# Routing of the first mixture of experts: one plan of seven digits for all experts, and counting in pairs of token columns

## The chip, the cores and the metric

The kernel runs on one core of one Trainium2 chip. The metric is the time of one execution on the device, in microseconds (us).

## The reference

The program is a chain of three parts: attention in chunks, a mixture of experts with balanced routing, and a second mixture with the two best experts per token. The change is in the routing of the first mixture, on 3072 tokens and 8 experts that take 384 tokens each:

```python
logits = x @ w_gate                       # 3072 x 8
order = np.argsort(-logits.flatten())
for idx in order:                         # best pairs of token and expert first
    tok, e = idx // E, idx % E
    if assigned[tok] >= 0 or counts[e] >= cap:   # cap = 384
        continue
    assigned[tok] = e
    counts[e] += 1
for e in range(E):
    mask = assigned == e
    out[mask] = np.maximum(x[mask] @ w1[e], 0.0) @ w2[e]
```

## The kernel before

**Stages.** Attention runs from 0 to some 112 us and leaves the logits `L` in SBUF: token n lies in partition n % 128 and column n // 128, so a tile has `G` = 24 columns of 128 tokens, for each of `E` = 8 experts. Then the first mixture runs expert by expert (`moe1`): `mm1` multiplies the expert's 384 gathered tokens by `w1` in three half-precision passes (products `m<-xT,w_...`), and for the first five experts `mm2_f32` multiplies by `w2` in single precision (products `m2f<-st,hT`). The second mixture (`moe2`) follows.

**Order of the work.** The order is written out when the kernel is built. `Pipe` keeps a modelled time for each engine; the main products call `tick()` between them, and generators (routing, lists, gathers, weight splits) that have come due by the modelled time issue their instructions there. `pipe.due` tells the splits of weights on VectorE when the routing wants VectorE next. Each engine then takes its instructions in that order, and waits in it. If a thing that the main products need isn't ready by the model, spare products `m<-ones` are put in.

**Routing.** `route` (a generator) finds, expert by expert, which expert fills up next, and at which logit. The logit is found digit by digit, as a number in bits. A round for digit s: VectorE compares the best logit `V` of each token with the candidates of the digit (`GE`, a 0/1 table of 24 columns by `nj` candidates); TensorE multiplies `GE` with the one-hot table `OH` of the tokens' best experts and so counts, for each candidate and expert, the tokens above (`cross`); VectorE compares the counts with the places left (`capB`, the flag `fl`); TensorE sums the flags over the candidates and spreads the sum to all partitions (`dg`); VectorE takes the largest (`d`) and makes the next candidates `ci`.

There are two plans. `FAST` has seven digits of 4, 3, 5, 5, 5, 5 and 5 bits and one token column per product: 24 products with 8 moving columns each. Expert 0 (which has its first two digits from a histogram made during attention, so five rounds are left) and expert 1 (seven rounds) use it. `THRIFTY` has eight digits of 4 bits and eight token columns per product: 3 products with 120 stationary and 64 moving columns, of which only the diagonal blocks are wanted. ScalarE evicts the result to `blk`, and eight products with slices of the identity add the blocks up. Experts 2 to 6 use it. Expert 7 needs no rounds. In the trace all PSUM tiles of the routing are called `rps`, and the flags `flf` (FAST) and `flt` (THRIFTY).

When an expert's threshold is known, `lists1` writes its list of tokens (`l1pos`, `slps`, `idx`), `gather1` fetches the rows by an indirect DMA on GpSimd's queue, and they are transposed, for experts 0 and 1 by TensorE (`tps`). Weights of expert k are fetched once its number is known (`est`), and split into two halves by ScalarE and VectorE. Nearly all instructions show line 68, the helper that records them, so they are told apart by their tiles.

Of the kernel before, what the change touches and what calls it, by code (L numbers as in the profile page):

```python
# [8 lines left out]
F32 = mybir.dt.float32  # L9
# [17 lines left out]
G = NTOK // 128  # L27
# [28 lines left out]
class Eng:  # L56


    def __init__(self, eng, pipe, name):
        self._a = (eng, pipe, name)  # L60
# [543 lines left out]
class Plan:  # L604


    def __init__(self, name, bits, cols):
        self.name, self.cols = name, cols
        self.shifts = [sum(bits[i + 1 :]) for i in range(len(bits))]
        self.nj = [(1 << b) - 1 for b in bits]  # L610
        self.off = [sum(self.nj[1:i]) for i in range(1, len(bits) + 1)]
# [4 lines left out]
FAST = Plan("f", (4, 3, 5, 5, 5, 5, 5), 1)  # L616
THRIFTY = Plan("t", (4,) * 8, 8)
NJ, NT, NH = 31, 15, 127


def route_setup(ctx, pool):
# [13 lines left out]
    for plan in (FAST, THRIFTY):  # L635
        fl = pool.tile([max(plan.nj), len(plan.nj), E], BF16, name="fl" + plan.name)
        memset(fl, 0.0)
        setattr(ctx, "fl" + plan.name, fl)
    return [
        lambda: memset(ctx.capB, float(CAP)),  # L640
# [123 lines left out]
def route(ctx):  # L764
# [36 lines left out]
    for k in range(E):  # L801
        def tl(shape, dt, n, **kw):
            return pool.tile(shape, dt, tag="rt" + n, name=f"{n}_{k}", **kw)
# [24 lines left out]
        plan = FAST if k < 2 else THRIFTY  # L828
        jtab = getattr(ctx, "jtab" + plan.name)
        off, NS = plan.off, len(plan.nj)  # L830
        FL = getattr(ctx, "fl" + plan.name)
        score = tl([128, E], F32, "score")
        R = tl([128, FAST.off[-1] + 1], I32, "R")[:, : off[-1] + 1]
# [34 lines left out]
        for s in range(s0, NS):  # L868
            nj, o = plan.nj[s], off[s]
            GE = tl([128, G * NJ], F16, "GE")[:, : G * nj].rearrange("p (c j) -> p c j", j=nj)  # L870
            step = G if k else G // 2
            for c in range(0, G, step):
                bc = [128, step, nj]
                V_.tensor_tensor(
                    GE[:, c : c + step], V[:, c : c + step].unsqueeze(2).to_broadcast(bc),
                    cand[:, :nj].unsqueeze(1).to_broadcast(bc), op=ALU.is_ge,
                )
# [14 lines left out]
            g = plan.cols  # L892
            cross = pst([g * nj, E, g])
            for c in range(0, G, g):
                P_.matmul(
                    cross.rearrange("p e c -> p (e c)"), GE[:, c : c + g].rearrange("p c j -> p (c j)"), OH[:, :, c : c + g],
                    start=(c == 0), stop=(c == G - g),
                )
# [7 lines left out]
            cnt = cross[:, :, 0]  # L906
            if g > 1:
                pipe.due = pipe.rdy("s", cross) + 900
                yield pipe.rdy("s", cross) - 200
                blk = tl([NT * THRIFTY.cols, E, THRIFTY.cols], F16, "blk")  # L910
                pipe.S.activation(blk, cross, AF.Copy)
                pipe.due = pipe.rdy("p", blk) + 450
                yield pipe.rdy("p", blk)
                cnt = pst([nj, E])
                for i in range(g):
                    P_.matmul(
                        cnt, ctx.id16[: g * nj, nj * i : nj * i + nj], blk[:, :, i], start=(i == 0), stop=(i == g - 1)
                    )
            pipe.due = pipe.rdy("v", cnt)
            yield pipe.due - 200  # L920
            fl = FL[:nj, s]
            V_.tensor_tensor(fl, cnt, capB[:nj], op=ALU.is_ge)
# [23 lines left out]
            else:  # L946
# [3 lines left out]
                ci = tl([128, NJ], I32, "ci")  # L950
# [94 lines left out]
def constants():  # L1045
# [10 lines left out]
    for plan in (FAST, THRIFTY):  # L1056
        jtab = [np.arange(1, n + 1) << sh for n, sh in zip(plan.nj[1:], plan.shifts[1:])] + [np.zeros(1)]
        f["jtab" + plan.name] = np.tile(np.concatenate(jtab).astype(np.int32), (128, 1))
# [1043 lines left out]
```

## Time and profile before

| | |
|---|---|
| median of 3 runs | 1035.27 us (1031.76 to 1038.93) |
| the profiled execution | 1030.15 us, span 1028.4 us |
| TensorE products busy | 980.4 us, 95% of the span |
| VectorE busy | 639.3 us, 62% |
| ScalarE busy | 466.5 us, 45% |
| GpSimd busy | 283.9 us, 28% |
| mean granted clock of TensorE | 0.980 |

Busy times of TensorE are those of pipelined products: several are under way at once, so what a group of products costs is read from the starts of its neighbours, not from its own duration. In the rows, PE is TensorE (PEld its weight loads), DVE is VectorE, ACT is ScalarE, POOL is GpSimd. A shape such as `128*31 128x8` is 128 rows by 31 stationary columns, with a result of 8 moving columns per row of the moving side.

### The profile page before, as it was taken

What the parts mean: (1) busy time and instruction counts of PE and PEld (TensorE: products, weight loads), DVE (VectorE), ACT (ScalarE), POOL (GpSimd) and SP (SyncE); (2) the same over time, 40 slices, a digit from 0 to 9 for tenths busy, and PEclk for the clock granted to TensorE, in tenths of its full rate; (3) what the DMA queues carried; (4) which work ended last, traced back from release to release, by engine and by line L of the source; (5) the groups of instructions that cost most, each with busy time, mean ns of one, the idle gap of its engine ahead of it and who ended that gap; (6) DMA issues with size and microseconds to landing.
All of it is one profiled execution on the core that took longest, in us unless ns stands there. A gap on an engine that the chain in (4) does not pass through costs nothing. (4 is left out here: it accounts for less than half of the span.)

```text
span 1028.4 us, 21808 instructions
## 1 busy us (share of the span) xinstructions
PE 980.4 (95%) x8278; PEld 590.8 (57%) x8278; DVE 639.3 (62%) x2095; ACT 466.5 (45%) x799; POOL 283.9 (28%) x468
## 2 busy tenths in 40 slices
PE   7988589899999999999989999999999999999997
PEld 5777467676767675545554454555545555555553
DVE  5998776566665958697756845547355464554221
ACT  5776252643461738888225635044161441523110
POOL 3776042010111304030022333133232432332321
PEclk8999689999999999999999999999999999999999
DMA  8888564466858678778187829458186492654410
GB/s 308 299 276 276 195 221 151 129 190 175 229 181 201 166 211 225 232 228 149 37 257 219 244 72 301 84 155 244 62 250 132 117 290 63 182 116 102 123 62 31
DMA packets 146848, 184.61 MB, mean 180 GB/s; under 512 B 105154, under 2 KB 105666, under 8 KB 145204
## 3 DMA queue, kind: packets, MB, share of 16 engines
q1 hardware_dynamic: 129410, 131.73, 45.4%
q0 software_dynamic: 13872, 45.15, 15.1%
q10 hardware_dynamic: 3458, 6.30, 1.7%
q8 instruction: 66, 1.08, 0.5%
q14 instruction: 42, 0.34, 0.1%
HBM read 127.10 MB, written 32.44 MB: 155 GB/s over the span
## 5 line engine op out<-in xcount | busy, mean ns | idle before, releaser
L68 PEld LDWEIGHTS <-hT 128*128 128x128 f16 (+2 forms) x1800 | 143.2, 99 | 158.2 <-issue 2.8
L68 ACT ACTIVATE hT<-m 128x384 f16<-128x384 f32 (+2 forms) x152 | 75.6, 499 | 275.7 <-PE m L68 274.1
L68 DVE SCALAR_TENSOR_TENSOR hT<-m,hT 128x384 f16<-128x384 f32 (+2 forms) x152 | 86.4, 570 | 97.9 <-ACT hT L68 97.8
L68 ACT ACTIVATE junk<-st 128x1024 f16<-128x1024 f32 x108 | 113.6, 1052 | 56.2 <-DMA st<-w_dram 29.0
L68 PE MATMUL m2f<-st,hT 128*128 128x256 f32 x480 | 127.6, 398 | 0.6 <-ACT hT L68 0.6
L68 POOL DMA_INDIRECT out_dram<-pv,ts x47 | 48.6, 1034 | 250.2 <-DVE pv L68 88.7
L68 DVE SCALAR_TENSOR_TENSOR pv<-m,ys,pv 128x512 f32<-128x512 f32 (+2 forms) x47 | 33.5, 714 | 118.3 <-PE m L68 118.2
L68 PE MATMUL m<-xT,w_0h 128*128 128x384 f16 (+2 forms) x384 | 96.6, 331 | 2.9 <-DMA xT<-xg 2.9
L68 PE MATMUL m<-xT,w_2h 128*128 128x384 f16 (+2 forms) x384 | 97.7, 334 | 1.7 <-DVE hT L68 1.7
L68 PE MATMUL m<-xT,w_3h 128*128 128x384 f16 (+2 forms) x384 | 96.7, 332 | 0.0
L68 PE MATMUL m<-xT,w_1h 128*128 128x384 f16 (+2 forms) x384 | 96.5, 331 | 0.0
L68 PEld LDWEIGHTS m2f<-st,hT 128*128 128x128 f32 x480 | 83.3, 190 | 10.2 <-ACT hT L68 1.0
L68 PE MATMUL m<-w_3h,hT 128*128 128x512 f16 (+2 forms) x300 | 71.6, 345 | 1.4 <-DVE hT L68 1.4
L68 PE MATMUL m<-w_0h,hT 128*128 128x512 f16 (+2 forms) x300 | 72.1, 346 | 0.0
L68 PE MATMUL m<-w_1h,hT 128*128 128x512 f16 (+2 forms) x300 | 71.5, 345 | 0.0
L68 PE MATMUL m<-w_2h,hT 128*128 128x512 f16 (+2 forms) x300 | 71.5, 345 | 0.0
L68 PE MATMUL m<-xT,w_2l 128*128 128x384 f16 (+2 forms) x192 | 64.2, 334 | 0.0
L68 PE MATMUL m<-xT,w_1l 128*128 128x384 f16 (+2 forms) x192 | 63.6, 331 | 0.0
L68 PE MATMUL m<-xT,w_3l 128*128 128x384 f16 (+2 forms) x192 | 63.5, 331 | 0.0
L68 PE MATMUL m<-xT,w_0l 128*128 128x384 f16 (+2 forms) x192 | 63.5, 331 | 0.0
L68 POOL DMA_INDIRECT xg<-x,rows x54 | 54.2, 1004 | 28.1 <-issue 12.7
L68 POOL DMA_INDIRECT pv<-out_dram,tg x47 | 46.5, 990 | 55.1 <-DMA out_dram<-pv,ts 39.0
(350 smaller groups left out, 1829.3 us busy)
## 6 DMA issues: line engine op xcount, KB each, us to landing
st<-w_dram SPq DMA_DIRECT2D x64, 512.0 KB
st<-x_dram SPq DMA_DIRECT2D x64, 512.0 KB
v<-vctx_dram SPq DMA_DIRECT2D x24, 520.0 KB
k<-kT_dram SPq DMA_DIRECT2D x24, 312.0 KB
xr<-rb SPq DMA_DIRECT2D x24, 264.0 KB
x<-rb SPq DMA_DIRECT2D x24, 264.0 KB
q<-qT_dram SPq DMA_DIRECT2D x12, 512.0 KB
out_dram<-zero ACTq DMA_DIRECT2D x24, 256.0 KB
```

Of the source, the lines that this page charges most:

```text
L68: return f(*args, **kw)
```

## The change

The plans become one, the seven digits of `FAST`, for all experts. Token columns are counted in pairs: the candidates of a column lie 32 apart in a constant tile `GE`, so that a pair is a stationary side of 64 columns (31 candidates, one unused, 31 candidates, one unused) and a moving side of 16. Twelve such products add up in one PSUM tile of 64 rows. Rows 0 to 30 at the even columns hold the counts of the even token columns, rows 32 to 62 at the odd ones those of the odd token columns. VectorE adds the two in the test: `need` is the places left less the odd counts, and the flag is whether the even counts reach `need`. ScalarE's eviction `blk` and the eight products that add the blocks go.

```diff
-FAST = Plan("f", (4, 3, 5, 5, 5, 5, 5), 1)
-THRIFTY = Plan("t", (4,) * 8, 8)
-NJ, NT, NH = 31, 15, 127
+PLAN = Plan((4, 3, 5, 5, 5, 5, 5))
+NT, NH, PAIR = 15, 127, 32
...
+    ctx.fl = pool.tile([max(PLAN.nj), len(PLAN.nj), E], BF16, name="fl")
+    memset(ctx.fl, 0.0)
+    ctx.GE = pool.tile([128, G, PAIR], F16, name="GE")
     return [
+        lambda: memset(ctx.GE, 0.0),
...
-        plan = FAST if k < 2 else THRIFTY
-        jtab = getattr(ctx, "jtab" + plan.name)
+        plan, jtab, FL = PLAN, ctx.jtab, ctx.fl
...
-            GE = tl([128, G * NJ], F16, "GE")[:, : G * nj].rearrange("p (c j) -> p c j", j=nj)
+            GE = ctx.GE
             step = G if k else G // 2
             for c in range(0, G, step):
                 bc = [128, step, nj]
                 V_.tensor_tensor(
-                    GE[:, c : c + step], V[:, c : c + step].unsqueeze(2).to_broadcast(bc),
+                    GE[:, c : c + step, :nj], V[:, c : c + step].unsqueeze(2).to_broadcast(bc),
                     cand[:, :nj].unsqueeze(1).to_broadcast(bc), op=ALU.is_ge,
                 )
...
-            g = plan.cols
-            cross = pst([g * nj, E, g])
-            for c in range(0, G, g):
+            cross = pst([2 * PAIR, E, 2])
+            flat = cross.rearrange("p e c -> p (e c)")
+            for c in range(0, G, 2):
                 P_.matmul(
-                    cross.rearrange("p e c -> p (e c)"), GE[:, c : c + g].rearrange("p c j -> p (c j)"), OH[:, :, c : c + g],
-                    start=(c == 0), stop=(c == G - g),
+                    flat, GE[:, c : c + 2].rearrange("p c j -> p (c j)"), OH[:, :, c : c + 2],
+                    start=(c == 0), stop=(c == G - 2),
                 )
...
-            cnt = cross[:, :, 0]
-            if g > 1:
-                pipe.due = pipe.rdy("s", cross) + 900
-                yield pipe.rdy("s", cross) - 200
-                blk = tl([NT * THRIFTY.cols, E, THRIFTY.cols], F16, "blk")
-                pipe.S.activation(blk, cross, AF.Copy)
-                pipe.due = pipe.rdy("p", blk) + 450
-                yield pipe.rdy("p", blk)
-                cnt = pst([nj, E])
-                for i in range(g):
-                    P_.matmul(
-                        cnt, ctx.id16[: g * nj, nj * i : nj * i + nj], blk[:, :, i], start=(i == 0), stop=(i == g - 1)
-                    )
-            pipe.due = pipe.rdy("v", cnt)
+            pipe.due = pipe.rdy("v", cross)
             yield pipe.due - 200
-            fl = FL[:nj, s]
-            V_.tensor_tensor(fl, cnt, capB[:nj], op=ALU.is_ge)
+            fl, need = FL[:nj, s], tl([PAIR, E], F32, "need")[:nj]
+            odd = slice(PAIR, PAIR + nj)
+            V_.scalar_tensor_tensor(need, cross[odd, :, 1], -1.0, capB[odd], op0=ALU.mult, op1=ALU.add)
+            V_.tensor_tensor(fl, cross[:nj, :, 0], need, op=ALU.is_ge)
```

The table of candidates in the constants (`jtab`) is stored once in place of twice.

## Rows read from the trace of the kernel before

**Rows 1.** Busy time by stretch: length, then each engine's busy us, clock, DMA.

```profile
107.00:110.00 3.00, 2.00 (x20) 1.90 (x19) 0.87 (x5) 2.54 (x7) 0.00 (x0) 1.00 1.04 392
111.00:126.00 15.00, 6.42 (x134) 5.04 (x134) 13.29 (x56) 1.95 (x3) 2.08 (x13) 0.50 0.37 139
143.00:383.00 240.00, 236.11 (x1883) 163.70 (x1882) 159.90 (x679) 106.92 (x208) 36.71 (x87) 1.00 0.62 177
```

**Rows 2.** Waits of TensorE after 143 us: us in total, times, longest.

```profile
PE tps L68 <- DMA xg<-xr,idx: 2.6, 1, 2.6
...
PE rps L68 <- ACT blk L68: 0.7, 1, 0.7
```

**Rows 3.** Timeline of TensorE, second half of an expert: start us, us, instructions.

```profile
231.21 1.97 PE L68 MATMUL m2f<-st,hT 128*128 128x256 f32 x8
...
236.41 0.30 PE L68 MATMUL rps<-OH,GE 128*120 128x64 f16 x3
236.55 1.11 PE L68 MATMUL m2f<-st,hT 128*128 128x256 f32 x4
...
239.05 1.56 PE L68 MATMUL m2f<-st,hT 128*128 128x256 f32 x6
240.45 0.30 PE L68 MATMUL rps<-OH,GE 128*120 128x64 f16 x3
```

**Rows 4.** The same timeline in the first half of expert 0, during expert 1's routing.

```profile
148.35 0.33 PE L68 MATMUL m<-xT,w_1l 128*128 128x384 f16 x1
...
148.84 0.33 PE L68 MATMUL m<-xT,w_1l 128*128 128x384 f16 x1
149.10 0.80 PE L68 MATMUL rps<-OH,GE 128*31 128x8 f16 x24
149.83 0.50 PE L68 MATMUL m<-xT,w_1h 128*128 128x384 f16 x2
...
150.74 0.17 PE L68 MATMUL rps<-flf,onesb 31*128 31x8 bf16 x1
150.85 0.34 PE L68 MATMUL m<-xT,w_1l 128*128 128x384 f16 x1
```

**Rows 5.** The same timeline in the first half of expert 1, during expert 2's routing.

```profile
198.65 0.30 PE L68 MATMUL rps<-OH,GE 128*120 128x64 f16 x3
...
202.17 0.30 PE L68 MATMUL rps<-OH,GE 128*120 128x64 f16 x3
```

**Rows 6.** Instructions on the tile blk: count, ns min/median/max, first and last start.

```profile
L68 ACT ACTIVATE blk<-rps x40: 201/223/224, 177.2 to 373.6; 120x64 f16<-120x64 f32 x40
```

**Rows 7.** Timeline of TensorE in the second mixture, first products of 64 columns.

```profile
520.98 0.59 PE L68 MATMUL m<-w_3h,hT 128*128 128x512 f16 x2
521.41 0.38 PE L68 MATMUL m<-w_3l,hT 128*128 128x512 f16 x1
521.72 0.41 PE L68 MATMUL m<-w_0h,hT 128*64 128x256 f16 x4
```

**Rows 8.** Timeline of weight loads, histogram of expert 0, 127 columns.

```profile
108.59 0.32 PEld L507 LDWEIGHTS <-ge 128*127 128x127 f16 x4
110.58 0.18 PEld L507 LDWEIGHTS <-ge 128*127 128x127 f16 x1 [1.68 <-DVE ge L500]
111.32 0.40 PEld L507 LDWEIGHTS <-ge 128*127 128x127 f16 x3 [0.56 <-issue]
```

**Rows 9.** Timeline of all engines in a routing round of expert 0.

```profile
115.53 0.19 DVE L68 SCALAR_TENSOR_TENSOR ci<-d,R 128x31 int32<-128x31 int32 x1
...
115.75 1.00 DVE L68 TENSOR_TENSOR GE<-V,ci 128x372 f16<-128x372 f32 x2
...
116.36 0.95 PE L68 MATMUL rps<-OH,GE 128*31 128x8 f16 x24 [1.06 <-DVE GE L68]
```

**Rows 10.** Timeline of TensorE in the first half of expert 5.

```profile
393.92 0.76 PE L68 MATMUL slps<-slr,sloh 128*32 128x12 f16 x24
...
396.66 0.48 PE L68 MATMUL m<-xT,w_2h 128*128 128x384 f16 x2 [1.72 <-DVE hT L68]
```

More of the change, by code (lines that the diff above doesn't have):

```diff
@@ L604, with __init__ @@
 class Plan:
-    def __init__(self, name, bits, cols):
-        self.name, self.cols = name, cols
+    def __init__(self, bits):
         self.shifts = [sum(bits[i + 1 :]) for i in range(len(bits))]
@@ L634, in route_setup @@
     memset(ctx.left, float(CAP))
[L635 to L638, printed above, removed]
+    ctx.fl = pool.tile([max(PLAN.nj), len(PLAN.nj), E], BF16, name="fl")
+    memset(ctx.fl, 0.0)
+    ctx.GE = pool.tile([128, G, PAIR], F16, name="GE")
     return [
+        lambda: memset(ctx.GE, 0.0),
         lambda: memset(ctx.capB, float(CAP)),
@@ L827, in route @@
             return
-        plan = FAST if k < 2 else THRIFTY
-        jtab = getattr(ctx, "jtab" + plan.name)
+        plan, jtab, FL = PLAN, ctx.jtab, ctx.fl
         off, NS = plan.off, len(plan.nj)
-        FL = getattr(ctx, "fl" + plan.name)
         score = tl([128, E], F32, "score")
-        R = tl([128, FAST.off[-1] + 1], I32, "R")[:, : off[-1] + 1]
+        R = tl([128, off[-1] + 1], I32, "R")
         d = tl([128, 1], I32, "d", bufs=2)
@@ L949, in route @@
                     V_.tensor_reduce(score, dgs.rearrange("p s e -> p e s"), axis=AX.X, op=ALU.add)
-                ci = tl([128, NJ], I32, "ci")
+                ci = tl([128, PAIR], I32, "ci")
                 V_.scalar_tensor_tensor(
@@ L1055, in constants @@
     f["cand0"] = np.tile(np.where(k0 >= 0, k0, k0 ^ 0x7FFFFFFF).astype(np.int32).view(np.float32), (128, 1))
-    for plan in (FAST, THRIFTY):
-        jtab = [np.arange(1, n + 1) << sh for n, sh in zip(plan.nj[1:], plan.shifts[1:])] + [np.zeros(1)]
-        f["jtab" + plan.name] = np.tile(np.concatenate(jtab).astype(np.int32), (128, 1))
+    jtab = [np.arange(1, n + 1) << sh for n, sh in zip(PLAN.nj[1:], PLAN.shifts[1:])] + [np.zeros(1)]
+    f["jtab"] = np.tile(np.concatenate(jtab).astype(np.int32), (128, 1))
     k0 = (np.arange(1, NH + 1, dtype=np.int64) - 64) << 25
```

## The prediction

> **What bounds the kernel now.** I read three views in this order. First the busy time by stretch [rows 1]: from 143 to 383 us, where the first mixture of experts runs beside the routing of experts 1 to 6, TensorE is busy for 236.1 of 240 us at a granted clock of 1.00, VectorE for 159.9 and ScalarE for 106.9. So in that stretch a microsecond of TensorE work is a microsecond of the kernel, and the eviction that the change takes from ScalarE is not what the stretch waits for. From 111 to 126 us the picture is turned round: VectorE is busy for 13.3 of 15 us, TensorE for 6.4 at the lower clock (0.50, 1.2 GHz). That is the routing of expert 0, a chain of short instructions with nothing else to run. Then the waits of TensorE [rows 2]: the routing's own are small, 0.7 us for the eviction `blk`, and 2.6 us for the rows that expert 1's list gathers. Last the order of the instructions on TensorE, to see what one routing round costs the main stream.
>
> **What a round costs TensorE today.** The main products are the yardstick. In the second half of an expert (`m2f`) one takes 0.215 us: eight last 1.97 and four 1.11, so 0.86/4 [rows 3]. From one counting group at 236.41 to the next at 240.45 pass 4.04 us, with 14 `m2f` in them (4, 4 and 6): 4.04 - 14 x 0.215 = 1.03 us are the round's. In the first half (`mm1`) three products start in 0.49 us (148.35 to 148.84), so 0.163 each [rows 4]. From 198.65 to 202.17 there are 17 of them: 3.52 - 2.77 = 0.75 us [rows 5]. The 40 evictions `blk` from 177.2 to 373.6 us [rows 6] mark the rounds of experts 2 to 6 (five of eight); in TensorE's order 23 of them start within `m2f` and 17 within `mm1`: 23.7 + 12.8 = 36.5 us.
>
> Expert 1 uses one column per product. Its 24 products hold up the `mm1` stream by 149.83 - 148.84 - 0.163 = 0.83 us [rows 4]. They are spaced by (0.80 - 0.17)/23 = 0.027 us, 0.65 together; the other 0.18 us is lost at the group's edges. The flag's product costs 150.85 - 149.83 - 5 x 0.163 = 0.21 us.
>
> **What a round will cost.** Every round becomes 12 products with 64 stationary columns. Do they lose time at the edges, as the 31 do? The second mixture has a row: a first product of 64 columns comes 0.31 us after its forerunner, where (521.41 - 520.98)/2 = 0.215 is the rule [rows 7], so 0.095 is lost there too. I keep 0.18 for both edges. Spacing: no row has 64 columns with a short moving side. From below it is 0.027 [rows 4]. From above there are 127 columns at clock 1.00: four loads last 0.32 us; if one alone lasts 0.18 they are 0.05 apart, if nothing, 0.08 [rows 1, 8]. I take 0.06, half of it for 64 columns: 0.03. A group in `mm1` then costs 0.18 + 12 x 0.03 = 0.54 us, a round with its flag 0.75. In `m2f` the three groups of a round cost 1.03 - 0.75 = 0.28 more than in `mm1`, 0.09 each; two groups are left, so 0.75 + 0.18 = 0.93. Thirty-five rounds (five experts of seven) in about the same mix, 20 and 15, cost 18.6 + 11.3 = 29.9 us: 6.6 less than today. Expert 1 saves 7 x (0.83 - 0.54) = 2.0 us. With the spacing at 0.027 the two together save 10.1; at 0.06 the 42 groups cost 12 x 0.03 x 42 = 15.1 us more than in my sum, and the two lose 6.5.
>
> The Trainium skill, "TensorE: Matmul & The Clock Gate", section "LDWEIGHTS (loading the stationary operand)", says that a load takes its column count over 1.2, in ns, whatever the rows. That is 53 ns for 64 columns, so that the columns of two tokens in one product would cost as much as in two products. At clock 1.00 the loads of 127 columns came 50 to 80 ns apart, not 106 [rows 8], and I go by them; by the page the 42 groups would be some 12 us dearer than in my sum.
>
> **Expert 0.** Its five rounds lie on a bare chain, so every delay counts. The two halves of `GE` take 1.00 us from 115.75, and the products start at 116.36, after the first half [rows 9]; the last twelve wait for the second half. There will be six in their place. At this clock 127 columns take (0.40 - 0.18)/2 = 0.11 us [rows 8], so 64 about 0.055, and six of those last as long as twelve of 0.027: no gain. If they ran at 0.027 the gain were 6 x 0.027 = 0.16 us a round. `need` is added in front of the flag, and an instruction that reads the one before it starts 0.22 us after it (`GE` behind `ci`) [rows 9]. So +0.06 to +0.22 us a round; the first needs a spacing that this clock's rows speak against, so I take 0.2: +1.0 us.
>
> **The rest.** The wait for `blk` goes: -0.7 us [rows 2]. VectorE gets wider `GE` (31 digits, at most 1.00 us by the two halves) and `need`: at most 25 x 1.00 + 35 x 0.22 = 33 us on its 159.9 of 240, less what the eighth rounds took [rows 1, 9]. That keeps it at about 80% or under, so I put it at nothing, hidden behind the main products; if that cover is gone, splits of weights come late and TensorE waits. The constant `GE` tile, its memset on GpSimd and the smaller table of constants are put at nothing too: they fall in the attention stage, ahead of the routing. No DMA of the routing changes but that table.
>
> The routing of experts 2 to 6 loses a round each, and a hop in every round, so it ends earlier. Today the last list's products (393.92) run beside the first expert whose activations VectorE halves, and TensorE waits 1.72 us for VectorE soon after, at 396.66 [rows 10]. With the lists gone from there I expect that wait to go: -1.7 us, where the bounds are 0 and -1.7. Next late there would be ScalarE, whose work in that place stays.
>
> **Sum.** -6.6 - 2.0 + 1.0 - 0.7 - 1.7 = -10.0 us. The profiled execution took 1030.2 us (a span of 1028.4 and 1.8 around it), so 1020.2 by its own time; it lies 0.5% under the median of the runs, 1035.3. On the median: **1025.3**.
>
> **Rivals.**
> - *TensorE's gain comes back as waits.* For: the gather of expert 1 is already awaited for 2.6 us [rows 2], and a TensorE that gets there 2 us sooner waits 2 us longer if list and gather don't move. Against: that is the only wait for a list of this stage. If all of the 8.6 us come back, and the wait at 396 stays, the 1.0 is added and the 0.7 taken: 1035.6. If half: 1031.3.
> - *More is gained.* If the wait for expert 1's gather goes too (-2.6) and the spacing is 0.027 (-1.5): 1025.3 - 4.1 = 1021.2. For: expert 1's rounds hold 12 products less. Against: what is awaited in the end is a DMA.
> - *Pairs don't pay* (the change doesn't do what it says): 64 columns take 0.055 us at the full clock too, as I reckon for the lower one. Then 12 x 0.025 x 42 = 12.6 us are added to the sum: 1037.9, no faster. Against: [rows 8].
> - *Slower, by late flags.* TensorE takes its queue in order, and behind the flag's product stand main ones. That product stands 0.84 us behind the counting group at expert 1 (149.90 to 150.74) [rows 4]; VectorE has that long for the flag, and now has one instruction more in it, 0.22 us, behind whatever else it has been given. If all 42 flags are late by t, the loss is 42 t: from 0.24 us on the gain of 10 is eaten, and at 0.5 us the kernel takes 1025.3 + 21 = 1046.
>
> **Chances.** The forecast 0.47, gain given back 0.24, more gained 0.14, pairs that don't pay 0.07, late flags 0.08. The forecast's own range is 1020 to 1030. About 1% is what a measurement of this kernel can tell from no change: under 1024.9 is faster, over 1045.6 slower. Half of the forecast (0.24) and all of the greater gain (0.14) lie under the first: 0.38. Slower is late flags and a little of VectorE's cover failing: 0.09. The rest, 0.53, is within 1%. The range takes in the forecast, the greater gain and the gain given back, 1015 to 1037; pairs that don't pay and late flags, 0.15, are left out.
>
> **What would show it.** From 143 us on: groups of 12 products of 128x64 that hold up `mm1` by 0.54 us (spacing 0.03), no `blk`, 35 rounds in place of 40, and a stage that ends some 9 us sooner. At expert 0: rounds that are 0.2 us longer. Wrong would be: a spacing of 0.05 us or more at clock 1.00; flag products on TensorE with idle time in front of them that VectorE's flag ended; a wait for expert 1's gather that grew by as much as was saved; or TensorE waiting for splits of weights in the first mixture.

## The result: slower by half a per cent, and where the profile shows it

The changed kernel takes 1038.17 us (median of 21 runs, 1034.56 to 1046.22) where the kernel before took 1033.02 beside it (21 runs): a ratio of 1.0058, 95% interval 1.0043 to 1.0073. Measured again (a_again, six runs beside twelve) it is 1.0058 (1.0039 to 1.0077). The forecast was a gain of 10 us, and 1038.17 lies above the top of its range too. For scale: a mere copy of the kernel before, timed in the same way, came out at 1.0024 (1.0010 to 1.0039). So a ratio is read here only to about a quarter of a per cent: one that lies nearer to 1 than that shows nothing, even where its interval leaves 1 out.

The profiled execution has a span of 1036.4 us (before: 1028.4). Busy time by stretch, columns as in [rows 1], first the changed kernel, then its profile from the second measurement (a_again):

```profile
143.00:383.00 240.00, 235.50 (x1953) 166.85 (x1951) 178.72 (x724) 100.35 (x167) 42.16 (x99) 0.99 0.67 185
383.00:500.00 117.00, 112.16 (x694) 61.48 (x693) 81.09 (x238) 91.51 (x156) 15.06 (x49) 0.99 0.67 185
```

```profile
143.00:383.00 240.00, 237.33 (x1948) 169.34 (x1946) 176.69 (x716) 101.02 (x170) 42.25 (x98) 1.00 0.66 182
```

VectorE has 18.8 us more to do in this stretch than in [rows 1] (178.7 for 159.9), ScalarE 6.6 us less. The waits of TensorE, as in [rows 2], in the first profile of the changed kernel:

```profile
PE rps L68 <- DVE GE L68: 6.4, 6, 1.7
PE m L68 <- DVE hT L68: 4.7, 3, 2.1
PE dup L68 <- DVE lsh L68: 3.7, 4, 2.7
...
PE rps L68 <- DVE fl L68: 2.2, 5, 0.4
...
PE tot L68 <- ACT junk L68: 1.8, 1, 1.8
...
PE m L68 <- issue: 1.3, 3, 0.4
```

Of the two waits of [rows 2] neither is left: not the one for `blk`, nor the 2.6 us for expert 1's gather. (The waits for `GE`, but for 0.5 us, and the five for `fl` belong to expert 0's bare chain.) New are a wait for sums of squares (`tot`) and three named issue, which mean that TensorE waited for nothing that the profile shows. The wait for a list's product in the second mixture (`dup`) has grown: in the kernel before it is 0.8 us, none of its three over 0.3.

Waits alone don't explain the loss, since what is missing by the planner's model is bridged with spare products. So I divided the span at the first product of each stage in TensorE's timeline. A unit of the second mixture runs from its first product `m<-xT` to that of the next. In us, for the kernel before (b_third, its third profile) and four others:

| | before | changed | changed, again | e13_last | e17_last_dup |
|---|---|---|---|---|---|
| first product of expert 0 at | 141.50 | 144.20 | 141.18 | 142.64 | 142.37 |
| experts 0 to 4, whole | 238.18 | 243.85 | 240.49 | 233.29 | 233.27 |
| of this, first half of expert 1 | 20.17 | 29.90 | 28.36 | 18.43 | 18.43 |
| experts 5 to 7 | 101.75 | 103.32 | 102.39 | 102.55 | 104.22 |
| second mixture, first two units | 76.57 | 74.30 | 75.83 | 75.94 | 72.52 |
| from there to the last stage | 444.85 | 447.99 | 445.01 | 445.18 | 444.67 |

Three profiles of the kernel before put the five experts at 238.2, 239.6 and 240.5 us: most of the difference is the wait for the gather of expert 1 (1.0, 1.9 and 2.6 us). The first half of expert 1 is 20.17 to 20.18 in all of them. In the changed kernel it is 8 to 10 us longer, and all other halves of the five experts together are 5.9 us shorter in the second profile (212.1 for 218.0). That one stage is where the changed kernel loses.

Two things limit what this table can say. First, a wait can cost more than its length. In two profiles of the kernel before, b_again and b_third, TensorE waits 1.72 us for `hT` at the same place of expert 5. These are the wait and the 4 us behind it, in the one and in the other:

```profile
395.91 0.49 PE L68 MATMUL m<-xT,w_2h 128*128 128x384 f16 x2 [1.72 <-DVE hT L68]
...
396.00:400.00 4.00, 4.00 (x16) 2.00 (x16) 2.44 (x5) 1.58 (x4) 3.21 (x6) 0.60 1.01 283
```

```profile
393.06 0.49 PE L68 MATMUL m<-xT,w_2h 128*128 128x384 f16 x2 [1.72 <-DVE hT L68]
...
393.10:397.10 4.00, 4.00 (x25) 2.40 (x25) 3.38 (x6) 1.63 (x4) 3.34 (x6) 1.00 0.99 262
```

In b_again TensorE gets through 16 products there, at a mean granted clock of 0.60 (the lower level, 1.2 GHz, for most of it), in b_third through 25 at 1.00. Experts 5 to 7 take 103.43 us in b_again and 101.75 in b_third: that stretch is the difference. In the table, one such stretch each lies in 29.90 (clock 0.58 from 221 to 225 us, behind the wait for `tot`), in 103.32, 102.39 and 104.22 of experts 5 to 7 and in 76.57, 75.83 and 75.94 of the two units; 20.17, 28.36 and 18.43 hold none. So stages with a wait in them are compared to within 2 us only, and the loss is read from 28.36. Second, "changed, again" is the fastest of its six runs (1029.24 us, where their median is 1032.49). Its stages add up to 2.0 us more than those of "before", but the medians of that measurement lie 5.1 us apart. The clock is the likely home of most of the rest: it was 0.9762 in the mean of those six runs and 0.9805 in the twelve of the kernel before, which is 0.0043 x 1027 = 4.4 us at most, an estimate that takes all clock that isn't granted for lost time.

This is TensorE in the stage that loses, in the first profile:

```profile
208.92 0.33 PE L68 MATMUL m<-xT,w_2l 128*128 128x384 f16 x1
209.18 0.55 PE L68 MATMUL rps<-OH,GE 128*64 128x16 f16 x12
209.65 0.84 PE L68 MATMUL m<-ones 128*128 128x128 f16 x12
...
211.37 1.96 PE L68 MATMUL m<-ones 128*128 128x128 f16 x32
...
215.80 0.49 PE L68 MATMUL m<-xT,w_3h 128*128 128x384 f16 x2
...
219.78 0.16 PE L68 MATMUL tot<-sq,onesb 128*128 128x4 bf16 x1 [1.77 <-ACT junk L68]
```

From 209.65 to 215.80 it runs spare products (91 of them) between the products of the routing and of a list; the main products of `w_3`, the last quarter of expert 1's weight, begin at 215.80, 20.4 us into the stage. In the kernel before they begin 15.1 us into it:

```profile
209.55 0.33 PE L68 MATMUL m<-xT,w_3h 128*128 128x384 f16 x1
```

What they wait for is on VectorE, here in the changed kernel:

```profile
202.56 0.73 DVE L68 SCALAR_TENSOR_TENSOR w_3l<-st,s,w_3h 128x512 f16<-128x512 f32 x1
...
214.48 0.73 DVE L68 SCALAR_TENSOR_TENSOR w_3l<-st,s,w_3h 128x512 f16<-128x512 f32 x1
```

The low part of `w_3` is made in two halves, and the second comes 11.9 us behind the first. The eight halves of this weight lie between 190.15 and 214.48, one or two in a routing round, and then none while expert 2's threshold is closed, its list made and expert 3's rounds begun. In the kernel before they lie together, seven of them in one round and the eighth right behind its flag, at 192.97:

```profile
187.40 0.53 DVE L68 TENSOR_TENSOR GE<-V,ci 128x360 f16<-128x360 f32 x1
187.85 0.23 DVE L68 SCALAR_TENSOR_TENSOR R<-d,R 128x76 int32<-128x76 int32 x1
188.00 1.41 DVE L68 SCALAR_TENSOR_TENSOR w_0l<-st,s,w_0h 128x512 f16<-128x512 f32 x2
189.32 1.41 DVE L68 SCALAR_TENSOR_TENSOR w_1l<-st,s,w_1h 128x512 f16<-128x512 f32 x2
190.65 1.41 DVE L68 SCALAR_TENSOR_TENSOR w_2l<-st,s,w_2h 128x512 f16<-128x512 f32 x2
191.97 0.74 DVE L68 SCALAR_TENSOR_TENSOR w_3l<-st,s,w_3h 128x512 f16<-128x512 f32 x1
192.88 0.15 DVE L68 TENSOR_TENSOR flt<-rps,capB 15x8 bf16<-15x8 f32 x1 [0.17 <-PE rps L68]
```

That is one routing round, from its comparison `GE` to its flag `flt`, and it lasts 5.5 us, because ScalarE has the eviction `blk` behind four conversions of the same weight and a copy to `xT`:

```profile
185.94 1.14 ACT L68 ACTIVATE w_0h<-st,s 128x1024 f16<-128x1024 f32 x1
...
189.06 1.14 ACT L68 ACTIVATE w_3h<-st,s 128x1024 f16<-128x1024 f32 x1
190.10 1.00 ACT L68 ACTIVATE xT<-tps 128x1024 f16<-128x1024 f16 x1
191.00 0.21 ACT L68 ACTIVATE blk<-rps 120x64 f16<-120x64 f32 x1
```

So the eviction that the change removes was, at this place, a pause of the routing, and the weight was split in that pause. That was the theory to test (A, order). Its rival (B, load): the wider comparisons and the second operation of the flag simply fill VectorE.

### The profile page after: what moved, and what is told of

Read it like the earlier page. It is cut to its first block, busy times and chain, and to the rows that moved or that the text cites. A ratio compares the mean times of both kernels' runs of the same rounds, so it can differ in the third digit from the quotient of the medians.

```text
span 1036.4 us, 21628 instructions
## 1 busy us (share of the span) xinstructions
PE 982.5 (95%) x8203; PEld 594.7 (57%) x8203; DVE 652.0 (63%) x2116; ACT 459.2 (44%) x759; POOL 284.7 (27%) x470
## 5 line engine op out<-in xcount | busy, mean ns | idle before, releaser
L68 PE MATMUL m2f<-st,hT 128*128 128x256 f32 x480 | 119.9, 392 | 1.8 <-ACT hT L68 1.8
L68 PEld LDWEIGHTS m2f<-st,hT 128*128 128x128 f32 x480 | 85.9, 190 | 12.5 <-ACT hT L68 2.1
```

The costliest lines, as they stand in the source:

```text
L68: return f(*args, **kw)
```

## Experiments

Ratios are against the kernel before, timed beside it on the same chip, with their 95% intervals. All kernels compute the whole result. The first four edit the changed kernel.

**e1_yield.** Hold the routing back while halves are pending.

```diff
+            if k > 1 and ctx.pending:
+                pipe.due = 1e12
+                yield lambda: not ctx.pending
...
         S_.activation(hi, src, AF.Copy, scale=sj)
+        ctx.pending += 1
...
         done.append((hi, lo))
+        ctx.pending -= 1
```

> The changed kernel; the routing of experts 2 to 6 alone is held back before each of its rounds for as long as second halves of a weight split are still to be made on VectorE, so that those halves run in one block again. Nothing is left out of the computation. Theory A (order: without ScalarE's eviction the routing keeps VectorE round after round, the last half of expert 1's w_3 comes at 214.48 us where it came at 202.56 from its first half, and the first stage of expert 1 takes 29.90 us in place of 20.18): that stage comes back to 20 to 22 us and the kernel gains 6 to 10 us on the changed one, 1028 to 1032 us. Theory B (load: comparisons of 31 candidates at 0.93 us and the extra operation per round are simply more work than VectorE has room for in that stage): holding the routing back only moves the idle time, to the lists of expert 2 or a later stage, and the time stays within 3 us of 1038.

The eight halves run together again (186.90 to 191.55), the stage takes 18.96 us, the five experts 236.08. The ratio is 1.004 (1.0022 to 1.0058): little of it arrives. The profile shows another wait in this order, 4.0 us of TensorE for the transposed rows `yT` at 397.84. The stage is as A has it; the time, 1037.23 us, is within 3 us of 1038, as B has it.

**e2_hop.** Put ScalarE's copy back, with seven digits and pairs kept.

```diff
+            if k > 1:
+                pipe.due = pipe.rdy("s", cross) + 900
+                yield pipe.rdy("s", cross) - 200
+                blk = tl([2 * PAIR, E, 2], F32, "blk")
+                pipe.S.activation(blk, cross, AF.Copy)
+                cross = blk
             pipe.due = pipe.rdy("v", cross)
```

> The changed kernel; for experts 2 to 6 ScalarE copies each round's counts from PSUM to SBUF again, and VectorE's two operations for the flag read the copy: seven digits and counts in pairs stay, only the pause of the eviction comes back. Nothing is left out of the computation. Theory A (order): the routing of expert 2 waits behind ScalarE's conversions as it did before (4.2 us from the round's products to the next there), the halves run in the pauses, the first stage of expert 1 takes 20 to 23 us, and the kernel is at 1028 to 1033 us. Theory B (load): VectorE has as much to do as in the changed kernel; the stage stays at 28 us or more and the time at 1036 to 1040.

The halves lie together, 184.85 to 189.87, the stage takes 19.18 us, the ratio is 1.001 (0.999 to 1.003). B expected 28 us or more: it falls as the sole cause. The pause alone suffices for the stage, with VectorE as full as in the changed kernel (busy for 180.9 us from 143 to 383, where it was 178.7).

**e4_eight.** Eight digits of four bits for experts 2 to 6, pairs and no eviction.

```diff
+EIGHT = Plan((4,) * 8)
...
-        plan, jtab, FL = PLAN, ctx.jtab, ctx.fl
+        plan, jtab, FL = (PLAN, ctx.jtab, ctx.fl) if k < 2 else (EIGHT, ctx.jtab8, ctx.fl8)
```

> The changed kernel; experts 2 to 6 use eight digits of four bits (15 candidates a round, the plan of the kernel before) with the counts in pairs and without ScalarE's eviction. Nothing is left out of the computation. Theory B (load): a round's comparison is back at about 0.53 us from 0.93, so VectorE has its room again, the first stage of expert 1 falls to 20 to 23 us and the kernel to 1029 to 1034. Theory A (order): a round without a pause still keeps VectorE from the halves; the stage stays at 27 to 31 us, and with one round more per expert the time is 1037 to 1041 us.

The stage takes 19.01 us, the ratio is 1.001 (0.9992 to 1.0028). Here A missed: there is no pause, and the stage is whole. The halves are spread as in the changed kernel (187.22 to 200.13), but the last falls into one of the last rounds, 7.0 us into the stage.

**e7_gpsimd.** Let GpSimd take halves of expert 1.

```diff
-        idle = lambda: k == 0 and pipe.t["g"] <= pipe.clock + SLACKG
+        idle = lambda: k <= 1 and pipe.t["g"] <= pipe.clock + SLACKG
```

> The changed kernel; GpSimd may take second halves of the splits of expert 1 too when it has nothing to do (so far only those of expert 0). Nothing is left out of the computation. Theory A (order) and theory B (load) both expect the first stage of expert 1 to shrink from 29.90 us, since the last half need not wait for VectorE: to 20 to 23 us and the kernel to 1028 to 1033 us. If the stage stays at 28 to 30 us although the halves are made early, the late split was not what TensorE lacked, and both theories fall. A GpSimd that slows VectorE would show as halves on GpSimd several times as long as the 1.2 us of VectorE's and longer VectorE operations beside them.

The last half starts at 203.57 on GpSimd, 9.2 us into the stage, which takes 18.79; the ratio is 0.9975 (0.9953 to 0.9998). (A half takes 0.73 us on VectorE, not the 1.2 of the expectation.) GpSimd does slow VectorE: of the comparisons of 31 candidates (744 columns) from 143 to 383 us, the 6 that ran beside a half on GpSimd took 1.15 us (median, up to 1.90), the other 24 took 0.94.

**e3_vevict and e6_onecol** come from the other side: the kernel before, with VectorE as the evicting engine, and with the seven-digit, one-column plan for all experts.

```diff
-                pipe.due = pipe.rdy("s", cross) + 900
-                yield pipe.rdy("s", cross) - 200
+                pipe.due = pipe.rdy("v", cross)
+                yield pipe.due - 200
                 blk = tl([NT * THRIFTY.cols, E, THRIFTY.cols], F16, "blk")
-                pipe.S.activation(blk, cross, AF.Copy)
+                V_.tensor_copy(blk, cross)
```

> The kernel before; only the eviction of each round's counts for experts 2 to 6 is made by VectorE in place of ScalarE (eight digits, eight columns per product, the eight selecting products all stay). Nothing is left out of the computation. Theory A (the eviction's wait behind ScalarE's conversions was the pause in which VectorE split expert 1's weights): without it the halves spread over the routing rounds here too, spare products appear in the first stage of expert 1 and it grows from 20.18 us to 27 us or more, the kernel to 1037 to 1042 us. Theory B (the comparisons of 31 candidates and the second flag operation are the load that starved the splits): with comparisons of 0.53 us nothing is starved, that stage stays at 19 to 21 us and the time within 2 us of before.

```diff
-        plan = FAST if k < 2 else THRIFTY
+        plan = FAST
```

> The kernel before; experts 2 to 6 use the plan that experts 0 and 1 have there already, seven digits and 24 products of one column per round, with no eviction. So the counts in pairs and the operation for need are left away from the change, the seven digits and the missing pause stay. Nothing is left out of the computation. Theory A and theory B both expect the late last half, as in the changed kernel: the first stage of expert 1 at 27 to 31 us. On top of it each of 35 rounds displaces 0.83 us of products in place of the pairs' 0.58 or 0.67, some 7 us, so 1040 to 1047 us. If that stage stays at 19 to 21 us, the second operation of the flag (need, some 0.2 us per round) was enough to tip it.

Both are misses for A, and e6 is one for B too: the stage takes 19.43 and 20.23 us. The ratios are 1.0039 (1.0016 to 1.0062) and 1.008 (1.0049 to 1.0111). In e6 the halves are spread over the rounds, 187.68 to 200.83, but the last comes 6.8 us into the stage, in time. So without the pause the halves do spread, as A says, and yet that costs nothing until the last one misses expert 2's last round. The changed kernel goes over that edge. What tips it there is small: e6 has the same wide comparisons and lacks the pairs and `need`. Which of these does it, the operation more in each round or the earlier end of the routing, was not told apart. Over the kernels the two sides lie well apart: last half 2.3 us into the stage (e3), 6.8 (e6), 7.0 (e4) or 9.2 (e7): 18.8 to 20.2 us; 19.1 us into it (changed, both profiles): 28.4 and 29.9.

**e13_last and b_late** give and take that lateness alone. In the changed kernel the last quarter's two halves go out at once; in the kernel before the last half is held back.

```diff
         fits = pipe.fits(129.0 + 1.04 * step)
+        if i == 2 and j == 3:
+            fits = lambda: True
```

> The changed kernel; the two halves of w_3 of expert 1 go onto VectorE as soon as their input is there, in place of when VectorE has time left, and nothing else is edited. Nothing is left out of the computation. If the late last half of this one weight is what the first stage of expert 1 waits for: the stage falls from 28.4 to 29.9 us to 19 to 22, and the kernel from a ratio of 1.0058 to between 0.996 and 1.001. If what VectorE pushed behind it is needed just as soon, another stage grows by what this one gives back, and the ratio stays over 1.003.

```diff
+            if i == 2 and j == 3 and a:
+                yield pipe.clock + 22000.0
             yield lambda: fits() or idle()
```

> The kernel before; the second half of w_3 of expert 1 is held back on VectorE by 22 us, and nothing else is edited: it comes about as late behind the stage's start as in the changed kernel. Nothing is left out of the computation. If that lateness alone costs what it seems to in the changed kernel, the first stage of expert 1 grows from 20.18 to 28 to 32 us with spare products in it, and the kernel is slower by 5 to 10 us, a ratio of 1.005 to 1.010. If the stages behind make it good, the stage grows and the ratio stays under 1.003.

```profile
197.60 0.73 DVE L68 SCALAR_TENSOR_TENSOR w_2l<-st,s,w_2h 128x512 f16<-128x512 f32 x1
198.26 1.40 DVE L68 SCALAR_TENSOR_TENSOR w_3l<-st,s,w_3h 128x512 f16<-128x512 f32 x2
```

That is VectorE in e13_last: both halves at 198.26, the stage 18.43 us, the five experts 233.29, and the ratio 0.998 (0.996 to 1.0001), from 1.0058. In b_late the half comes later than meant (30 us behind the first, since the 22 are modelled time):

```profile
218.97 0.73 DVE L68 SCALAR_TENSOR_TENSOR w_3l<-st,s,w_3h 128x512 f16<-128x512 f32 x1
```

The stage takes 35.04 us with 191 spare products, and the ratio is 1.011 (1.0085 to 1.0134), both above what was expected for a shorter delay: 14.9 us lost in the stage, some 11 in the whole. So one operation of 0.73 us that comes 12 us late costs about 8 us (e13), and one that comes 30 us late about 11. The cause of the lost stage is settled by these two.

**b_load.** The kernel before, each comparison of experts 2 to 6 made twice; the pause stays.

```diff
+                if k > 1:
+                    V_.tensor_tensor(
+                        tl([128, G, NT], F16, "twice"), V.unsqueeze(2).to_broadcast(bc),
+                        cand[:, :nj].unsqueeze(1).to_broadcast(bc), op=ALU.is_ge,
+                    )
```

> The kernel before; for experts 2 to 6 VectorE makes each round's comparison twice, the second time into a tile that nobody reads: 40 operations of about 0.53 us, some 21 us more work, where the change adds 19. ScalarE's eviction and its pause stay. Nothing is left out of the computation. Theory B (load): VectorE has no room for the halves here either, the first stage of expert 1 grows by 3 us or more, or the f16 stages wait longer for hT than their 3.1 us, and the ratio is 1.003 to 1.010. Theory A (order): the halves still run in the eviction's pause, that stage stays at 20 to 22 us, and the ratio is within 0.998 to 1.003.

Each theory is half right. The stage stays at 20.19 us, the halves lie between 185.56 and 192.24, as A says. But the ratio is 1.0052 (1.0036 to 1.0069), as B says of the sum: experts 5 to 7 take 104.69 us in place of 101.75, the second mixture's first two units 78.18 in place of 76.57. The five experts themselves take 238.45 us, as before, so the loss lies behind the stretch that got the work; some 1.7 us of it are again a stretch of lower clock (0.57 from 457 to 461 us) behind a wait for `hT`. So VectorE's time is not free, although it is busy for only 177 of the 240 us.

**b_gps and e11_gps6.** GpSimd's help in the kernel before; and its help for all experts up to 6 in the changed kernel (`k <= 6` in the line of e7).

> The kernel before with GpSimd's help for expert 1's second halves alone; its routing is as it was. Nothing is left out of the computation. It tells whether the gain of the changed kernel with this help (ratio 0.9975 and, with the shift, 0.9974) is the help's or the change's. If the help has nothing to mend here, since the halves run in one block in the eviction's pause: ratio 0.998 to 1.003 and the first stage of expert 1 at 19 to 21 us. If the help is worth 2 to 3 us by itself, 0.997 to 0.998, and the change with it is worth nothing.

> The changed kernel; GpSimd may take second halves of all experts' splits up to expert 6 when it is idle. Nothing is left out of the computation. VectorE was busy 178.7 us of the 240 from 143 to 383 us in the changed kernel and 159.9 before. If what is left of the change's cost is VectorE's load (theory B in its weaker form: hT late in the stages from 383 to 490 us, 4 us of waits), the load falls by some 10 to 20 us, those waits shrink and the kernel is at a ratio of 0.992 to 0.997. If GpSimd's gathers queue behind the halves, or the load was not what made hT late, it is at 0.997 to 1.003.

b_gps is slower, 1.0069 (1.0046 to 1.0092): what e7 wins over the changed kernel is not the help's own. Halves of the two engines beside each other in b_gps:

```profile
187.75 1.47 POOL L68 TENSOR_TENSOR w_1l<-st,w_1h 128x512 f16<-128x512 f32 x1
188.12 1.64 DVE L68 SCALAR_TENSOR_TENSOR w_1l<-st,s,w_1h 128x512 f16<-128x512 f32 x1
```

e11 is slower by far, 1.0186 (1.0153 to 1.0218). Of the 40 halves that VectorE had from 143 to 383 us it keeps 9, which should take 31 x 0.73 = 22.6 us off it; its load fell only to 174.4 us. Its 127 instructions that ran beside a half on GpSimd took 22 us longer in all than the shortest of their kind in the changed kernel, which eats up most of the relief. GpSimd's load rose to 106.3 us, and TensorE waited 3.5 us for `NQ`, 2.3 for a half on GpSimd and 8.4 for `hT`. B's cure was worse than the load.

**e17_last_dup and a_dup.** e13_last still stood short of the forecast. Its profile has this on TensorE and on VectorE, in the second mixture:

```profile
527.25 0.16 PE L68 MATMUL dup<-lsh,dup 64*128 64x3 f16 x1 [3.97 <-DVE lsh L68]
```

```profile
526.35 0.56 DVE L68 SCALAR_TENSOR_TENSOR hT<-m,hT 128x384 f16<-128x384 f32 x1 [4.14 <-ACT hT L68]
526.83 0.17 DVE L68 COPY six<-slps 128x21 f32<-128x21 f32 x1
527.03 0.16 DVE L68 CAST lsh<-six 64x3 f16<-64x3 f32 x1
```

The product needs `lsh`, and on VectorE `six` and `lsh` stand in the queue behind an `hT` that waits 4.14 us for ScalarE's part of it. Main products stand behind `dup` on TensorE. The edit puts `dup` 4 us later into TensorE's order, with e13's edit and without it.

```diff
         V_.tensor_copy(sh, six[:m, h])
-        yield pipe.rdy("p", sh)
+        yield pipe.rdy("p", sh) + 4000
```

> The changed kernel with w_3's two halves of expert 1 put onto VectorE at once (as in e13_last) and with the one small product of a list of the second mixture (dup) put 4 us later into TensorE's order. Nothing is left out of the computation. In e13_last TensorE waited 4.0 us for that product's input, because on VectorE it stood behind an hT operation that itself waited 4.14 us for ScalarE. If that wait is a matter of the order alone: the two units from 516 us on take 33 to 34 us in place of 37.43, and the ratio goes from 0.998 to 0.993 to 0.996. If the list's rows are needed as early as they come, the wait comes back at the next gather and the ratio stays at 0.997 to 0.999.

> The changed kernel with only that one product put 4 us later. Nothing is left out of the computation. In the two profiles of the changed kernel the wait for it was 2.7 and about 3 us (in those of the kernel before under 0.7). If it is part of what the changed kernel loses, and the late half of w_3 the rest: the ratio falls from 1.0058 to 1.002 to 1.004. If not, it stays at 1.005 to 1.007.

e17 comes to 0.9954 (0.9936 to 0.9973), 1022.0 us beside 1027.1: 0.46% less than the kernel before, about twice what the copy showed. a_dup comes to 1.0029 (1.001 to 1.0047), so the edit is worth some 3 us to the changed kernel (the two intervals just overlap; the wait itself was 2.7 and 3.0 us in its profiles). The second unit of the second mixture takes 33.68 us in place of 37.43 in e17. That these 3 us were lost by the change is not shown: the kernel before takes as long in those two units (74.4 to 76.6 us; the changed one 74.3 and 75.8), with a wait of its own there for a gather (`xT`, 2.9 to 4.1 us), and the edit was not tried on it.

**Pads and copies.** In the first profile of the changed kernel three waits named issue stand in dense runs of 32-column products, such as

```profile
737.38 0.22 PE L68 MATMUL m<-w_2h,hT 128*32 128x128 f16 x1
738.03 0.32 PE L68 MATMUL m<-w_2h,hT 128*32 128x128 f16 x7 [0.44 <-issue]
```

and the three stages that hold these runs are 0.8, 0.8 and 1.4 us longer, 3.1 us of the second mixture. Theory C laid them to the place of the instructions in TensorE's stream. b_pad adds 64 products of 8 columns to the kernel before, e9_gps_pad37 adds 37 to e7.

```diff
+        pad = ctx.m2.tile([128, 8], F32, tag="m2", name="pad")
+        for _ in range(64):
+            ctx.nc.tensor.matmul(pad, ctx.ones16, ctx.ones16[:, :8], start=True, stop=True)
```

> The kernel before with 64 products of 8 columns put in behind the gather of expert 0: they do nothing but move every later instruction on TensorE's stream by 128. Nothing is left out of the computation. Theory C (the 3 us that all changed kernels lose in the second mixture, in the dense runs of 32-column products at 17 us into three of its stages, come from where the stream's blocks fall there): the idle times of about 0.65 us named issue appear in some of those stages, and the second mixture from its third unit on takes 1 to 3 us more than 444.75; first mixture the same but for the pads' own 2 to 4 us; 1035 to 1039 us. If they have another cause in the change, that part stays at 444.75 +- 0.3.

> The changed kernel with GpSimd's help for expert 1's splits and with 37 products of 8 columns behind the gather of expert 0, which make the count of TensorE's instructions differ from that of the kernel before by 256. Nothing is left out of the computation. Theory C (place of the stream's blocks): the second mixture from its third unit on moves away from the 448.2 us that it takes without them, down to 445 if 256 instructions are what a block holds; the pads cost 1 to 2 us early; 1027 to 1031 us. If it has another cause, that part stays at 448.2 +- 0.3 and the kernel is at 1031 to 1033.

> The kernel before, unchanged, profiled on the chip of the runs beside it. Theory C said that the idle times named issue in the dense runs of 32-column products come with the place of the stream's blocks; the two calls so far speak for another reading: five kernels profiled on other chips showed them, four on one chip did not, b_pad with its instructions shifted by 128 among these. If they belong to the chip or the execution, the second mixture from its third unit on takes the same here, within 0.5 us, in this kernel and in the three beside it, be it 445 or 448. If they belong to the change, this kernel takes 444.8 and the changed ones 448.

> The changed kernel, unchanged, beside the kernel before on one chip. The order of instructions is fixed when the kernel is built, so the last half of w_3 must lie as late here as in the first profile (12 us behind its first half), the first stage of expert 1 take 29 to 30 us, and the ratio come out at 1.004 to 1.008. If that stage takes 20 us here, the first profile was a chance of one execution and the main theory falls.

> The kernel before, unchanged, once more, beside the two. The ratio is 0.998 to 1.002. Its stages tell how far two profiles of one order of instructions lie apart: the wait for the gather behind expert 0 was 2.6 and 1.9 us, that for the second mixture's gather 2.9 and 3.4; these two are expected to differ by 1 us or more, and the stages that wait for no transfer by under 0.3 us.

b_pad: 1.0022 (1.0007 to 1.0037), that part 444.96 us. e9: 0.9974 (0.9958 to 0.999), that part 445.22 where e7 had 448.20. C is not borne out: e1, e2, e4 and e7, all on one chip, took 447.6 to 451.1 us there; the fourteen other kernels, on two other chips, took 444.7 to 445.3, whatever their order, the changed kernel among them (a_again: 445.01, and no such wait; b_again: 444.95). So the 3.1 us of the first comparison of profiles are none of the change's. Whether chip or execution makes them was not told apart. a_again repeats the late half (199.54 and 211.47), the stage (28.36, a little under the 29 to 30 expected, without the stretch of lower clock) and the ratio. b_third, an unedited copy, is at 1.0024 where 0.998 to 1.002 was expected; of its stages the gather's wait differs most from b_again's (1.0 for 1.9 us), as expected, and experts 5 to 7, which wait for no gather, differ by 1.7 us, which was not: that is the stretch of lower clock shown above.

**Not settled.** Why e1 and e2, whose five experts are 2 to 4 us shorter than before, show no gain. Part of it is the clock: their profiles have two stretches of the lower level each in experts 5 to 7 (105.63 and 104.86 us, where b_third has none and takes 101.75), and over their twelve runs each the granted clock was 0.976 and 0.977 in the mean, beside 0.980 in the kernel before. In both, and in b_load, b_gps, e3 and e11, GpSimd's queue has, next to the first store that waits over 20 us in every kernel, a second store ahead of or between the second mixture's first gathers that waits 2 us or more for VectorE; here e2_hop, then e13_last, where the three gathers follow one another:

```profile
510.72 0.98 POOL L68 DMA_INDIRECT xg<-x,rows  x1 [1.53 <-DVE lmkey L68]
513.82 1.02 POOL L68 DMA_INDIRECT out_dram<-z,ts  x1 [2.12 <-DVE z L68]
515.14 0.98 POOL L68 DMA_INDIRECT xg<-x,rows  x1 [0.31 <-issue]
516.42 0.95 POOL L68 DMA_INDIRECT xg<-x,rows  x1 [0.30 <-issue]
```

```profile
506.19 0.98 POOL L68 DMA_INDIRECT xg<-x,rows  x1 [0.30 <-DVE lmgt L68]
507.48 0.95 POOL L68 DMA_INDIRECT xg<-x,rows  x1 [0.31 <-issue]
508.73 0.94 POOL L68 DMA_INDIRECT xg<-x,rows  x1 [0.30 <-issue]
```

Those six take 77.1 to 79.0 us for the second mixture's first two units, all other kernels 72.0 to 76.6. No run isolated it.

## Why the prediction was wrong, step by step

**Spacing of 64 columns: right.** 0.03 us was forecast; the starts of the 12 products lie 0.032 us apart at a granted clock of 1.00 (median of 451) and 0.054 at 0.50 (median of 55; forecast 0.055). The rows behind it, a group in `mm1` (weight loads, then products) and one of expert 0:

```profile
150.69 0.42 PEld L68 LDWEIGHTS <-GE 128*64 128x64 f16 x11 [0.32 <-DVE nt L68]
```

```profile
150.43 0.33 PE L68 MATMUL m<-xT,w_1l 128*128 128x384 f16 x1
150.69 0.55 PE L68 MATMUL rps<-OH,GE 128*64 128x16 f16 x12
151.17 0.50 PE L68 MATMUL m<-xT,w_1h 128*128 128x384 f16 x2
```

```profile
116.64 0.85 PEld L68 LDWEIGHTS <-GE 128*64 128x64 f16 x12 [1.16 <-DVE GE L68]
```

The Trainium skill, "TensorE: Matmul & The Clock Gate", section "LDWEIGHTS (loading the stationary operand)", gives 53 ns for 64 columns. That agrees with the rows at the lower level of the clock (1.2 GHz), not with those at the upper (2.4 GHz).

**The terms on TensorE: right in kind, the gain a fifth smaller.** A group displaces 151.17 - 150.43 - 0.163 = 0.58 us of `mm1` (forecast 0.54) and 0.67 of `m2f` (0.63); the flag's product 0.21 and 0.30. A round thus costs 0.79 and 0.98 us, where 0.75 and 0.93 was forecast. The 35 rounds gain 36.5 - 20 x 0.98 - 15 x 0.79 = 5.1 us in place of 6.6, expert 1 gains 7 x (0.83 - 0.58) = 1.8 in place of 2.0. The edges of a group were priced at 0.18 us by those of 31 columns; they are 0.20.

**Expert 0: right.** Its rounds last 2.63 us (`GE` at 116.04 and 118.67) where they lasted 2.42, so 0.21 more (0.2 forecast). As forecast, the pairs give nothing back at this clock: all products of a round last 0.94 us where [rows 9] has 0.95.

**The wait for `blk`: gone, as forecast. The wait at 396: not gone.** TensorE waits 2.03 us for `hT` in the same place (398.07) and once more at 431.87 and 434.50. The forecast laid that wait [rows 10] to the last list's products beside it; they have moved ahead (`slps` is no longer there) and the wait stays. So the term of -1.7 us came to nothing: it was a guess from nearness in time.

**VectorE at nothing: the step that failed.** The forecast saw "at most 33 us" more on VectorE, found that it would stay under 80% busy, and priced it at nothing, "hidden behind the main products; if that cover is gone, splits of weights come late and TensorE waits". The cover did go, at one place, and the forecast's last sign of being wrong (TensorE waiting for splits of weights in the first mixture) is what the runs showed, with spare products in the wait's place. The reason is one that a busy share doesn't show: the halves have no fixed place on VectorE, they run where the routing leaves room, and the room was the eviction's pause. The step compared sums over 240 us; what decides is a deadline (products of `w_3`, 15 us into one stage) and which of several claimants goes first in the 15 us before it. The price: 28.36 - 20.17 = 8.2 us in that stage. Mending it alone (e13) took the ratio from 1.0058 to 0.998, 8 us.

**The sum again.** -5.1 - 1.8 + 1.0 - 0.7 + 0 = -6.6 us from the change's own terms, +8.2 for the late half: +1.6 us, near the 2.0 of the stages. The ratio says 0.58% of 1033, 6.0 us. Of the 4 us between, a copy alone showed 0.24% (2.5 us), and the lower clock of the changed kernel's runs can hold up to 4.4; they were not told apart. With the late half mended and `dup` moved (e17) the ratio is 0.9954, -4.7 us, for the -6.6 of the terms.

**The rivals.** None named this. "Gain comes back as waits" was given 0.24 with expert 1's gather as the place; that wait vanished (2.6 us to nothing). Late flags were the slower rival, and from 143 us on TensorE waited for no flag in either profile of the changed kernel. The forecast of slower, 0.09, had "a little of VectorE's cover failing" in it and priced it at a little.

## What to carry to other kernels

When an edit takes a wait away from one chain, list what else runs in that wait on each engine, with the deadline of each piece, before calling it free. An engine that is busy for 75% of a stretch can still deliver one small operation 12 us late, if that operation has no rank of its own among its competitors; look up when its consumer needs it, and give it a rank. And profile an unedited copy: here it set the bar at a quarter of a per cent, showed that 3 us of the difference between the first two profiles belonged to no edit, and that a wait of the same length was followed by the lower clock in one execution and not in another.

## What the runs showed of the hardware

- Products of 64 stationary columns follow each other 0.032 us apart at a granted clock of 1.00 and 0.054 at 0.50, where 31 columns take 0.027 at 1.00 [rows 4] and, in expert 0's rounds of the kernel before, 0.027 at 0.50 too: at the upper level twice the columns cost a fifth more time, and half the products pay; at the lower level they don't.
- Behind the same wait of 1.72 us for `hT` the granted clock was 0.60 over the next 4 us in one execution of the kernel before (b_again) and 1.00 in another (b_third), and the stages around it took 1.7 us more in the first.
- Runs of 32-column products were slower, with waits named issue in them (0.44 us each in the changed kernel's first profile): the stages that hold them took 0.8 to 3.1 us longer there and in the four kernels on one chip (e1, e2, e4, e7), and at most 0.13 us longer in the fourteen on two other chips, with whatever order of instructions.
- A half of a split takes 0.73 us on VectorE and, as two operations, 0.85 + 1.3 us on GpSimd. VectorE's own instructions take longer beside them: a half 1.64 us in the rows of b_gps, a comparison of 744 columns 1.15 us in the median for 0.94 (e7). With 35 halves on GpSimd, ahead of `NQ` and `hT`, the kernel lost 1.9%.
